# A planned attention and expert kernel: another model of transfers in its planner, and another order on each engine

## The chip, the cores and the metric

The kernel runs on one core of one Trainium2 chip. Time is device time in microseconds (us), from runs of the whole program on that core. Five engines work beside each other, each through its own list of instructions in order: TensorE (PE), VectorE (DVE), ScalarE (ACT), GpSimd (POOL) and SyncE (SP). SP computes nothing; it issues the loads from device memory. ACT issues the stores, between its own computations.

## The reference

The input `x` has 4 batches of 11456 tokens with 128 features; there are 32 inducing points and 8 experts. Cut to what matters:

```python
def mab(q, kv):                       # softmax attention
    s = scale * (q @ kv.T); a = softmax(s); return a @ kv
h   = mab(inducing, x)                # per batch: 32 points look at all tokens
out = mab(x, h)                       # per batch: all tokens look at the 32 points
# then a mixture of experts on every token of out
expert = argmax(normalised(out) @ normalised(expert_emb).T / tau)
y = gate_weight * (relu(out @ w1[expert]) @ w2[expert])
```

The second step of a batch needs all of that batch's `h`, and `h` needs every token of the batch. So each batch has a point at which everything waits for the last of its loads.

## The kernel before

A batch is cut into six pieces `k` of 2048 tokens (the last has 1280 here and overlaps). Each piece is loaded twice: `xT` (or `xL` for the last piece) holds features on the partitions, `x` holds tokens on the partitions, and a small `xR` holds the last rest of 192 tokens of a batch. Batch 0 makes three of its `x` pieces on PE instead of loading them.

Stage 1 of a batch (`stage1`) computes scores of the inducing points against the pieces (L495), their running maximum (L556, L563), exponentials on ACT (L571), transposes on PE (L594), and sums weighted rows of `x` (L617). `finish` joins the sums into `hT`, the transposed `h` of the batch, lets an expert be picked (`pick`) and has SP load that expert's two weight matrices (`get_w`, L753 and L754). Stage 2 (`stage2`) scores each piece against `hT` (L792), which is the last use of that piece's `xT` buffer, and makes the exponentials and two groups of sums (L363, with tiles `HB` and `gbd`). `gate` makes the gate weights. `fold` folds the expert's two matrices into one small matrix `L`. Stage 3 (`stage3`) multiplies by the gate weights on POOL (L1150), makes the output on PE (L1169), copies it out of PSUM on ACT (L1176) and stores it from ACT (L445).

The four batches overlap: stage 1 of batch b+1 is worked in between stages 2 and 3 of batch b. Buffers are rings: seven `xT` of 1024 KB, two `xL` of 640 KB, four `x` of 1024 KB, one `xR` of 96 KB. A load waits on SP until the oldest buffer of its ring is free, and everything behind it on SP waits as well. `ORDER` holds for each engine the order of the operations, by their numbers. At build time `Plan.run` walks through these lists with estimated durations and places each operation in time; from that it takes the PSUM banks and the number of zero products (`fill`, L1265, a product of the zero tile `wz`) that are put into PE's estimated idle times. The times themselves do not reach the chip: there an instruction starts when its semaphores allow it.

Lines of this program that the text below touches: L461 loads `xT` and `xL`, L474 loads `x`, L480 loads `xR`, L724 reads the picked expert into a register of SP, L1303 issues four zero products at the start. The ring sizes and the six kinds of loads:

```python
BUFS = dict(xT=7, xL=2, x=4, xR=1, s1=2, pt=1, e=10, hq=2, ...)
nc.sync.dma_start(new(b)[:, a:a + w], st.xT_src(o + a, w))              # L461
nc.sync.dma_start(new(b)[:, :n], xP[st.b, :, 16 * k:16 * k + n, :])     # L474
nc.sync.dma_start(new(st.xr), xR[st.b])                                 # L480
nc.tensor.matmul(ps_all[:, b], lhsT=wz[:, 0:P], rhs=wz, start=True, stop=True)   # L1265, a zero product
```

Of the kernel before, what the change touches and what calls it, by code (L numbers as in the profile page):

```python
# [18 lines left out]
PE = mybir.EngineType.PE  # L19
ACT = mybir.EngineType.Activation  # L20
DVE = mybir.EngineType.DVE
# [42 lines left out]
    PE=(15, 18, 16, 29, 24, 28, 52, 31, 26, 53, 38, 42, 66, 40, 76, 48, 55, 62, 50, 86, 3, 72, 64, 82, 89, 74, 93, 84, 96, 139, 101, 126,  # L64
# [8 lines left out]
    Activation=(22, 0, 30, 25, 19, 35, 36, 39, 23, 54, 45, 37, 59, 46, 60, 49, 69, 79, 63, 70, 80, 47, 61, 71, 73, 91, 81, 92, 83, 95,  # L73
# [10 lines left out]
    DVE=(20, 21, 17, 57, 33, 34, 2, 27, 32, 43, 44, 58, 67, 77, 41, 68, 78, 56, 87, 51, 88, 65, 90, 94, 4, 75, 85, 97, 98, 102, 127, 128,  # L84
# [12 lines left out]
    SP=(5, 6, 9, 7, 10, 14, 12, 8, 11, 13, 124, 137, 254, 256, 125, 241, 103, 138, 161, 216, 382, 369, 162, 217, 242, 255, 383, 370, 501,  # L97
        462, 486, 406, 348, 461, 487, 499, 407, 614, 627, 500, 615, 746, 706, 628, 593, 651, 731, 744, 652, 707, 732, 745, 838, 1018,
        1025,),
    Pool=(1, 133, 157, 170, 237, 176, 250, 178, 276, 180, 111, 114, 282, 184, 186, 116, 284, 190, 191, 286, 193, 290, 292, 296, 201, 209,  # L100
# [11 lines left out]
class Buf:  # L112


    def __init__(self, ring, n=1):
        self.ring = ring
        self.n = n
        self.left = 0
        self.free_at = 0.0
        self.at = None  # L120
        self.t = None
# [5 lines left out]

class Plan:
# [7 lines left out]


    RATE = 405e3
    LANES = 8
    LANDING = 1.5  # L140
    BEGIN = 1.7
# [7 lines left out]
    MOST = 16  # L149

# [57 lines left out]
    def ready_at(self, o, clock):  # L208
# [5 lines left out]
        if o.size and len(self.under_way) >= self.LANES:  # L214
            t = max(t, self.under_way[-self.LANES] + self.HOP)
# [26 lines left out]
    def run(self):  # L242
        clock = {e: 0.0 for e in ENGINES}
# [3 lines left out]
        rest = [0.0, 0.0]  # L247
        at = 0.0
        left = {e: [self.ops[i] for i in ORDER[e.name]] for e in ENGINES}
        order = []  # L250
        while any(left.values()):
# [15 lines left out]
            if o.size:  # L267

                go = max(0.0, o.end + self.BEGIN - at) * self.RATE
                at = max(at, o.end + self.BEGIN)  # L270
                low = min(go / 2, *rest)
                rest = [r - low for r in rest]
                rest = [max(0.0, r - (go - 2 * low)) for r in rest]
                q = 0 if o.eng == SP else 1
                rest[q] += o.size
                o.end = o.done = at + (rest[q] + min(rest)) / self.RATE + self.LANDING
                self.under_way += [o.done] * o.parts
# [11 lines left out]
            order.append(o)  # L289
        for o in order:  # L290
            if o.spare:
                bank, idle = o.spare
                self.fill(bank, min(self.MOST, int((idle - self.SPARE) / self.FILL)))
            o.fn()
# [41 lines left out]
def tile_attn_moe(ctx: ExitStack, tc: tile.TileContext, xT, xP, xR, indT, emb, tau, w1, w2, aux, outT):  # L336
# [296 lines left out]
    def finish(plan, st):  # L633
# [110 lines left out]
        st.do["vp"] = c(DVE, 0.25, vp, free=[b6])  # L744
# [240 lines left out]
    def fold(plan, st):  # L985
# [23 lines left out]
        def signs():  # L1009
            ss = small.tile([P, NCH], F32, name="ss")  # L1010
            nc.vector.tensor_reduce(ss, st.G, AX.X, ALU.add)
            t["pos"] = small.tile([P, NCH], F32, name="pos")
            nc.vector.tensor_scalar(t["pos"], ss, 0.0, None, ALU.is_ge)
            t["ss"] = ss
        o_s = c(DVE, 0.6, signs)

        def chosen():
            st.Gm = bat.tile([P, NCH, M], F32, name="Gm")
# [404 lines left out]
```

## Time and profile before

| | us |
|---|---|
| median of 3 runs | 204.05 (203.6 to 205.35) |
| the profiled execution | 203.44 |
| its span, first to last instruction | 201.5 |
| PE busy | 180.0 (89%) |
| VectorE busy | 156.6 (78%) |
| ScalarE busy | 128.0 (64%) |
| GpSimd busy | 104.5 (52%) |
| moved by DMA | 72.32 MB, 359 GB/s over the span |

The granted clock of PE is 0.988 over the span. The profile's time lies 1.94 us above its span, and 0.6 us below the median. Of the 72.32 MB, 48.13 MB are read and 23.72 MB written. A chain of waits is read from its end back; a window gives each engine's busy time and what the transfers moved.

### The profile page before, as it was taken

How to read it: one execution, taken by the hardware profiler on the slowest of the kernel's cores; microseconds unless marked ns; L12 is line 12 of the kernel's file. 1: busy time of each engine (PE TensorE's matmuls, PEld its weight loads, DVE VectorE, ACT ScalarE, POOL GpSimd, SP SyncE). 2: the span in 40 equal slices, each digit the busy share in tenths (PEclk: the TensorE clock that was granted, in tenths of full speed). 3: DMA queues.
4: the chain of work that ended last, by engine and by line, in shares of the span. 5: the costliest groups of instructions: out<-in, count | busy, mean ns of one | idle time of the engine just before them, and what ended most of it. 6: DMA issues, size and time to landing. Idle time of an engine off the chain costs nothing.

```text
span 201.5 us, 6512 instructions
## 1 busy us (share of the span) xinstructions
PE 180.0 (89%) x2568; PEld 90.3 (45%) x2568; DVE 156.6 (78%) x446; ACT 128.0 (64%) x305; POOL 104.5 (52%) x178
## 2 busy tenths in 40 slices
PE   7999999999996999995979998897899999999940
PEld 2466853653575453334634453354543333433310
DVE  6148627999977899787659999699489999878830
ACT  2066960756796647965665967688587799874400
POOL 3010000048874823686456177789665889987500
PEclk9999999999999999999999999999999999999995
DMA  6999999999999999999995999999767966688991
GB/s 198 424 420 379 415 410 361 347 419 421 413 415 423 321 352 394 434 412 426 417 419 185 425 371 365 422 428 425 304 246 300 378 259 264 259 332 333 390 415 39
DMA packets 12227, 72.32 MB, mean 359 GB/s; under 512 B 1624, under 2 KB 2144, under 8 KB 4896
## 3 DMA queue, kind: packets, MB, share of 16 engines
q1 hardware_dynamic: 7984, 48.12, 60.6%
q10 hardware_dynamic: 4208, 23.75, 28.7%
q8 instruction: 21, 0.34, 0.7%
q14 instruction: 14, 0.11, 0.2%
HBM read 48.13 MB, written 23.72 MB: 357 GB/s over the span
## 4 chain that ended last, share of the span: by engine, by line
PE 48%; DMA 34%; POOL 5%; DVE 3%; ACT 3%; issue 2%; ACTq 0%; POOLq 0%; DVEq 0%; SPq 0%
DMA x<-in_xP 19%; DMA xT<-in_xT 16%; PE ps L363 9%; PE ps L792 8%; PE ps L617 7%; PE ps L1169 6%; PE ps L495 5%; PE ps L1265 5%; PE ps L594 3%; PE ps L522 3%; POOL e L1150 2%; PE ps L1303 1%; ACT o L1176 1%; PE ps L1071 1%; DVE nn L834 1%
## 5 line engine op out<-in xcount | busy, mean ns | idle before, releaser
L830 POOL TENSOR_TENSOR hq<-hq,e 128x512 f32<-128x512 f32 (+1 forms) x24 | 29.1, 1216 | 42.7 <-ACT hq L826 42.7
L1176 ACT COPY o<-ps 128x512 f32<-128x512 f32 (+1 forms) x78 | 40.9, 567 | 10.0 <-PE ps L1169 9.0
L1150 POOL TENSOR_TENSOR e<-e,fb 128x512 f32<-128x512 f32 (+1 forms) x24 | 28.9, 1210 | 4.6 <-DVE fb L1146 2.4
L1169 PE MATMUL ps<-e,L 32*128 32x512 f32 (+1 forms) x192 | 26.0, 610 | 0.5 <-POOL e L1150 0.3
L617 PE MATMUL ps<-x,pt 128*32 128x128 f32 x608 | 20.8, 274 | 4.4 <-DMA x<-in_xP 4.1
L363 PE MATMUL ps<-e,gbd 128*32 128x256 f32 (+1 forms) x384 | 24.1, 367 | 0.1
L363 PE MATMUL ps<-e,HB 128*32 128x512 f32 (+1 forms) x192 | 24.0, 568 | 0.1
L571 ACT ACTIVATE s<-ps,nb 128x1024 f32<-128x1024 f32 (+3 forms) x15 | 13.4, 895 | 16.3 <-DVE nb L563 12.8
L495 PE MATMUL ps<-xT,indT_sb 128*32 128x512 f32 x160 | 20.8, 598 | 2.7 <-DMA xT<-in_xT 2.7
L556 DVE TENSOR_REDUCE mk<-ps 128x1 f32<-128x1024 f32 (+3 forms) x15 | 14.0, 939 | 11.7 <-PE ps L495 10.1
L792 PE MATMUL ps<-xT,hT 128*32 128x512 f32 x160 | 20.3, 596 | 0.1
L617 PEld LDWEIGHTS ps<-x,pt 128*32 128x32 f32 x608 | 16.4, 109 | 8.8 <-DMA x<-in_xP 3.0
L814 ACT ACTIVATE e<-e 128x512 f32<-128x512 f32 (+1 forms) x24 | 14.6, 608 | 8.0 <-DVE R L809 7.8
L1265 PE MATMUL ps<-wz 128*128 128x512 f16 x71 | 18.9, 401 | 0.1
L363 PEld LDWEIGHTS ps<-e,gbd 128*32 128x32 f32 x384 | 12.1, 110 | 13.4 <-issue 5.0
L826 ACT COPY hq<-ps 128x512 f32<-128x512 f32 (+1 forms) x24 | 13.3, 555 | 6.4 <-PE ps L363 5.8
L834 DVE TRANSPOSE_TENSOR_REDUCE nn<-hq 128x16 f32<-128x512 f32 (+1 forms) x24 | 15.8, 662 | 1.9 <-POOL hq L830 1.8
L798 DVE TRANSPOSE_TENSOR_REDUCE mx<-ps 128x16 f32<-128x512 f32 (+1 forms) x24 | 15.6, 662 | 1.5 <-PE ps L792 0.9
L1146 DVE STREAM_TRANSPOSE fb<-f 128x512 f32<-128x512 f32 (+1 forms) x24 | 15.6, 655 | 0.8 <-POOL f L975 0.6
L803 DVE STREAM_TRANSPOSE e<-mx 128x512 f32<-128x512 f32 (+1 forms) x24 | 15.3, 650 | 0.1
L809 DVE CUSTOM_DVE_ANT_0 e<-e,ps 128x512 f32<-128x512 f32 (+1 forms) x24 | 15.1, 631 | 0.2
L594 PE MATMUL ps<-ident,s 128*128 128x128 f32 (+1 forms) x92 | 13.2, 280 | 1.6 <-issue 1.6
(190 smaller groups left out, 307.2 us busy)
## 6 DMA issues: line engine op xcount, KB each, us to landing
xT<-in_xT SPq DMA_DIRECT2D x20, 1024.0 KB, 11.6
out<-o ACTq DMA_DIRECT2D x18, 1024.0 KB, 5.5
x<-in_xP SPq DMA_DIRECT2D x17, 1024.0 KB, 10.8
xL<-in_xT SPq DMA_DIRECT2D x4, 640.0 KB, 12.8
x<-in_xP SPq DMA_DIRECT2D x4, 512.0 KB, 17.3
w1t<-in_w SPq DMA_DIRECT2D x4, 512.0 KB, 6.1
w2t<-in_w SPq DMA_DIRECT2D x4, 512.0 KB, 6.8
out<-x ACTq DMA_DIRECT2D x2, 1024.0 KB, 6.2
```

The costliest lines, as they stand in the source:

```text
L363: nc.tensor.matmul(out[q:q + M], lhsT=lhsT[:, q:q + M], rhs=rhs, start=start, stop=stop)
L495: nc.tensor.matmul(ps[32 * j:32 * j + 32, :].rearrange("p (g i) -> p g i", i=128), lhsT=indT_sb, rhs=v[:, j], start=True, stop=True)
L594: nc.tensor.transpose(ps[:tw, q:q + 128], s1.t[:, at[k] + c0:at[k] + c0 + tw], ident)
L617: nc.tensor.matmul(ph.t[32 * j:32 * j + 32, 0:C], lhsT=pt.t[:tw, tat[k] + g, 32 * j:32 * j + 32], rhs=x, start=k == ks[0] and g == 0, stop ...
L792: nc.tensor.matmul(ps[32 * j:32 * j + 32, :W].rearrange("p (t i) -> p t i", i=32), lhsT=st.hT[:, 0:M], rhs=v[:, j], start=True, stop=True)
L798: nc.vector.tensor_reduce(new(mx)[:, :T], b1.t[:, :W].rearrange("p (t i) -> p t i", i=32), AX.X, ALU.max, apply_transpose=True)
L830: nc.gpsimd.tensor_tensor(paired(hq.t[:, :W]), paired(hq.t[:, :W]), halved(e.t[:, :W]), ALU.mult)
L834: nc.vector.tensor_reduce(new(nn)[:, t0:t0 + T], hq.t[:, :W].rearrange("p (t i) -> p t i", i=32), AX.X, ALU.add, apply_transpose=True)
L1150: nc.gpsimd.tensor_tensor(e.t[:, :W], e.t[:, :W], fb.t[:, :W], ALU.mult)
L1169: nc.tensor.matmul(new(pcs[j])[:, :W], lhsT=st.L[32 * j:32 * j + 32, :], rhs=pf.t[32 * j:32 * j + 32, :W], start=True, stop=True)
L1176: (nc.vector.tensor_copy if dve else nc.scalar.copy)(v[:, j], pcs[j].t[:, :W].rearrange("c (t i) -> c t i", i=32))
L1265: nc.tensor.matmul(ps_all[:, b], lhsT=wz[:, 0:P], rhs=wz, start=True, stop=True)
```

## The change

Three things change. First, the planner's model of transfers: a class `Transfers` keeps one queue for SP and one for ACT, gives each an equal share of a fixed rate, moves the estimated landing of all transfers under way whenever one is added, and adds a delay that grows with the time for which the transfers have been busy (at most 2.4 us), for sixteen transfer engines that drift apart. PE's planned time now starts at 3.1 us and SP's at 1.0. Second, the first place for zero products is divided by 0.4 us in place of 0.22, and PE's first idle time is shorter, so there are 7 products there in place of 16; with all later places the program has 63 zero products where it had 75. Two estimated durations on DVE change, and these two wait for POOL in the plan. Third, `ORDER` holds another order for every engine. No computation is added or taken away other than zero products, and no buffer or tile changes size. The numbers of `ORDER` tell a reader little; a line of SP's stands for the rest:

```diff
-    SP=(5, 6, 9, 7, 10, 14, 12, 8, 11, 13, 124, 137, 254, 256, 125, 241, 103, 138, ...
+    SP=(5, 6, 9, 7, 10, 12, 8, 11, 14, 13, 124, 137, 138, 125, 254, 216, 161, 103, ...
...
+class Transfers:
+    RATE = 424e3
+    BEGIN = (1.4, 0.6)
+    LANDING = 0.8
+    DRIFT = 0.1
+    APART = 2.4
+    def add(self, o, t):
+        self.run(t)
+        q = 0 if o.eng == SP else 1
+        self.queues[q].append([o, o.size, o.end + self.BEGIN[q]])
+        Transfers(self).run(1e6)
+    def run(self, to):
+        while self.now < to:
+            on = [q for q in self.queues if q and q[0][2] <= self.now + 1e-9]
...
+            rate = self.RATE / len(on)
+            step = min([to - self.now, begin - self.now] + [q[0][1] / rate for q in on])
+            self.now += step
+            for q in on:
+                q[0][1] -= rate * step
+                if q[0][1] < 1:
+                    o = q.pop(0)[0]
+                    o.end = o.done = self.now + self.LANDING + min(self.APART, self.DRIFT * (self.now - self.busy))
...
-    RATE = 405e3
     LANES = 8
-    LANDING = 1.5
-    BEGIN = 1.7
+    CLOCK = {PE: 3.1, ACT: 0.0, DVE: 0.0, SP: 1.0, POOL: 0.0}
...
+    FILL0 = 0.4
...
-                self.fill(bank, min(self.MOST, int((idle - self.SPARE) / self.FILL)))
+                self.fill(bank, min(self.MOST, int((idle - self.SPARE) / (self.FILL if filled else self.FILL0))))
+                filled = True
...
-        st.do["vp"] = c(DVE, 0.25, vp, free=[b6])
+        st.do["vp"] = c(DVE, 0.4, vp, free=[b6], port=True)
...
-        o_s = c(DVE, 0.6, signs)
+        o_s = c(DVE, 0.68, signs, port=True)
```

Three places show what moved. The first is SP, the loads of batch 1 behind the first two `xT` pieces of that batch, before:

```order
L461 DMA xT<-in_xT 128x2048 x2
L461 DMA xL<-in_xT 128x1280
L480 DMA xR<-in_xR 48x512
L474 DMA x<-in_xP 128x2048
L461 DMA xT<-in_xT 128x2048
L724 TENSOR_LOAD ei
```

and the same place now (`ei` is the picked expert; the lines are those of the changed file, 36 higher):

```order
L497 DMA xT<-in_xT 128x2048 x2
L510 DMA x<-in_xP 128x2048 x2
L497 DMA xL<-in_xT 128x1280
L497 DMA xT<-in_xT 128x2048 x2
L760 TENSOR_LOAD ei
```

The `xR` of batch 1 is gone from here: it now stands as the 25th of SP's operations where it was the 14th, just ahead of the last `x` piece of that batch. Two `x` pieces and two `xT` pieces stand ahead of the reading of the expert, where there were one of each. In batch 2 the `xR` moves the same way, from the 29th to the 39th place.

The second place is SP again, between the last `x` piece of batch 2 and the reading of batch 2's expert, before:

```order
L474 DMA x<-in_xP 128x1024
L474 DMA x<-in_xP 128x2048
L480 DMA xR<-in_xR 48x512
L461 DMA xT<-in_xT 128x2048
L474 DMA x<-in_xP 128x2048
L724 TENSOR_LOAD ei
```

and now:

```order
L510 DMA x<-in_xP 128x1024
L510 DMA x<-in_xP 128x2048
L497 DMA xL<-in_xT 128x1280
L510 DMA x<-in_xP 128x2048
L497 DMA xT<-in_xT 128x2048 x2
L516 DMA xR<-in_xR 48x512
L760 TENSOR_LOAD ei
```

The `xR` of batch 3 goes behind an `xL`, an `x` and two `xT` pieces; the `xL` and one `xT` stood behind the expert's weights before.

The third place is PE in the last batch, towards the end of its stage 2, before (`e` are exponentials, `HB` and `gbd` the tables of that batch, `L` the folded matrix of batch 2):

```order
L363 MATMUL ps<-pad_135,ones 32x1 x4
L363 MATMUL ps<-e,gbd_137 32x256 x8
L363 MATMUL ps<-pad_135,ones 32x1 x4
L363 MATMUL ps<-e,HB 32x320 x4
L1169 MATMUL ps<-e,L 128x512 x4
L363 MATMUL ps<-Lp,sel_124 32x128 x4
```

and now:

```order
L399 MATMUL ps<-e,HB 32x512 x4
L1205 MATMUL ps<-e,L 128x512 x4
L1301 LDWEIGHTS wz
L1301 MATMUL ps<-wz 128x512
L399 MATMUL ps<-pad_135,ones 32x1 x4
L399 MATMUL ps<-e,gbd_137 32x160 x8
L1091 MATMUL ps<-ident,wo 1x128
L399 MATMUL ps<-e,HB 32x320 x4
```

Zero products now stand between the stage 2 products of the last batch: four of them ahead of its last `HB` product, and eight more ahead of batch 2's last output product. Before, the first of them there came behind the last stage 2 product, 12 in one place.

More of the change, by code (lines that the diff above doesn't have):

```diff
@@ L63 @@
 ORDER = dict(
-    PE=(15, 18, 16, 29, 24, 28, 52, 31, 26, 53, 38, 42, 66, 40, 76, 48, 55, 62, 50, 86, 3, 72, 64, 82, 89, 74, 93, 84, 96, 139, 101, 126,
[8 rows of a table removed]
-    Activation=(22, 0, 30, 25, 19, 35, 36, 39, 23, 54, 45, 37, 59, 46, 60, 49, 69, 79, 63, 70, 80, 47, 61, 71, 73, 91, 81, 92, 83, 95,
[10 rows of a table removed]
-    DVE=(20, 21, 17, 57, 33, 34, 2, 27, 32, 43, 44, 58, 67, 77, 41, 68, 78, 56, 87, 51, 88, 65, 90, 94, 4, 75, 85, 97, 98, 102, 127, 128,
[12 rows of a table removed]
-    SP=(5, 6, 9, 7, 10, 14, 12, 8, 11, 13, 124, 137, 254, 256, 125, 241, 103, 138, 161, 216, 382, 369, 162, 217, 242, 255, 383, 370, 501,
-        462, 486, 406, 348, 461, 487, 499, 407, 614, 627, 500, 615, 746, 706, 628, 593, 651, 731, 744, 652, 707, 732, 745, 838, 1018,
-        1025,),
-    Pool=(1, 133, 157, 170, 237, 176, 250, 178, 276, 180, 111, 114, 282, 184, 186, 116, 284, 190, 191, 286, 193, 290, 292, 296, 201, 209,
[4 rows of a table removed]
+    PE=(15, 16, 18, 28, 29, 31, 53, 52, 24, 42, 26, 38, 55, 66, 40, 48, 76, 62, 50, 72, 86, 64, 82, 89, 74, 93, 84, 3, 96, 139, 126, 99,
[8 rows of a table added]
+    Activation=(19, 22, 35, 54, 25, 0, 30, 39, 36, 45, 23, 37, 59, 49, 46, 69, 60, 70, 47, 63, 61, 79, 80, 73, 71, 81, 91, 92, 83, 95,
[10 rows of a table added]
+    DVE=(20, 21, 17, 33, 34, 57, 43, 44, 58, 32, 2, 67, 68, 56, 27, 77, 41, 78, 87, 51, 88, 65, 90, 75, 94, 85, 4, 97, 127, 98, 128, 100,
[12 rows of a table added]
+    SP=(5, 6, 9, 7, 10, 12, 8, 11, 14, 13, 124, 137, 138, 125, 254, 216, 161, 103, 241, 369, 162, 382, 217, 242, 256, 255, 499, 370, 383,
+        407, 487, 461, 406, 486, 348, 614, 462, 627, 501, 500, 615, 744, 628, 706, 651, 746, 593, 731, 707, 652, 732, 745, 1018, 838,
+        1025,),
+    Pool=(1, 133, 170, 157, 237, 176, 250, 276, 178, 114, 111, 180, 282, 186, 184, 284, 116, 190, 191, 286, 193, 292, 296, 209, 290, 201,
[4 rows of a table added]
 )
@@ L125, with __init__ @@
     pass
+class Transfers:
[4 more added lines that the diff above has]
+    APART = 2.4
+    def __init__(self, other=None):
+        self.queues = [[list(x) for x in q] for q in other.queues] if other else [[], []]
+        self.now, self.busy = (other.now, other.busy) if other else (0.0, None)
+    def add(self, o, t):
[6 more added lines that the diff above has]
+            on = [q for q in self.queues if q and q[0][2] <= self.now + 1e-9]
+            begin = min([q[0][2] for q in self.queues if q and q not in on], default=1e9)
+            if not on:
+                self.busy = None
+                self.now = min(to, begin)
+                continue
+            if self.busy is None:
+                self.busy = self.now
+            rate = self.RATE / len(on)
[6 more added lines that the diff above has]
+                    o.end = o.done = self.now + self.LANDING + min(self.APART, self.DRIFT * (self.now - self.busy))
+                    for b in o.free:
+                        b.free_at = max(b.free_at, o.done)
 class Plan:
@@ L214, in ready_at @@
         if o.size and len(self.under_way) >= self.LANES:
-            t = max(t, self.under_way[-self.LANES] + self.HOP)
+            t = max(t, self.under_way[-self.LANES].done + self.HOP)
         o.room = 0.0
@@ L242, in run @@
     def run(self):
-        clock = {e: 0.0 for e in ENGINES}
+        clock = dict(self.CLOCK)
         self.pool_from = 0.0
@@ L246, in run @@
         self.under_way = []
-        rest = [0.0, 0.0]
-        at = 0.0
+        dma = Transfers()
         left = {e: [self.ops[i] for i in ORDER[e.name]] for e in ENGINES}
@@ L267, in run @@
             if o.size:
[L269 to L277, printed above, removed]
+                dma.add(o, t)
+                self.under_way += [o] * o.parts
             for b in o.take:
@@ L289, in run @@
             order.append(o)
+        filled = False
         for o in order:
```

68 rows, old and new, of tables (Activation, DVE, PE, Pool) are left out of this document.

## The prediction, made before the result

> **What bounds the kernel now.** I read the page's head first, then the chain of waits in order of time, the transfers by windows, and SP's waits.
>
> ```profile
> span 201.5 us, 6512 instructions
> ...
> DMA packets 12227, 72.32 MB, mean 359 GB/s; under 512 B 1624, under 2 KB 2144, under 8 KB 4896
> ```
>
> The chain (start, duration, what):
>
> ```profile
> 1.39 1.89 PE ps L1303 x4
> ...
> 35.53 13.24 DMA xT<-in_xT
> ...
> 76.63 8.91 DMA xT<-in_xT
> 85.56 19.05 DMA x<-in_xP
> ...
> 104.65 1.00 PE ps L617 x24
> ...
> 117.14 9.48 DMA xT<-in_xT
> 126.68 18.44 DMA x<-in_xP
> ...
> 145.17 1.00 PE ps L617 x24
> 146.17 1.06 PE ps L1169 x5
> ```
>
> From 35 us to 145 us the chain runs through loads three times, and each time it ends at the PE work that needs them: at 104.65 the last weighted rows of batch 2, at 145.17 those of batch 3. Behind 145.17 no load of `x` or `xT` is left, and 56.3 us of work for the last batch follow to the end of the span at 201.5. So the end moves with the landing of the last `x`, as far as the engines keep up.
>
> A transfer that takes 19 us isn't slow; it stands behind others. The windows (us from the span's start: length, busy us of PE, PEld, DVE, ACT, POOL with counts, granted clock, busy share of the transfer engines, GB/s) show whether the transfers were full:
>
> ```profile
> 2.00:28.00 26.00, 25.77 (x327) 15.89 (x324) 13.50 (x64) 14.84 (x37) 0.89 (x5) 1.00 1.01 400
> 28.00:38.00 10.00, 9.86 (x132) 4.29 (x132) 7.71 (x23) 2.42 (x5) 0.00 (x0) 1.00 0.96 354
> 38.00:66.00 28.00, 25.96 (x473) 16.04 (x477) 24.77 (x67) 19.97 (x50) 18.08 (x31) 1.00 1.01 416
> 66.00:68.00 2.00, 1.99 (x30) 0.68 (x26) 2.00 (x5) 2.00 (x4) 1.10 (x3) 1.00 0.86 229
> 68.00:106.00 38.00, 33.72 (x557) 17.24 (x549) 29.88 (x81) 24.97 (x59) 21.02 (x35) 1.00 1.01 407
> 106.00:112.00 6.00, 5.99 (x92) 2.31 (x84) 5.78 (x15) 3.60 (x10) 3.99 (x4) 1.00 0.64 220
> 112.00:142.00 30.00, 26.87 (x414) 13.99 (x410) 26.93 (x69) 22.25 (x52) 20.84 (x35) 1.00 1.01 404
> ```
>
> They were, at 400 to 416 GB/s, except in three places: 28 to 38, 66 to 68 and 106 to 112 us. SP's own waits and issues tell why (waits: us in total, times, longest):
>
> ```profile
> SPq L480 <- PE ps L617: 25.4, 3, 12.2
> ...
> SPq L474 <- DMA x<-in_xP: 15.8, 3, 9.7
> ```
>
> ```profile
> 16.50 0.33 SPq L461 DMA_DIRECT2D xL<-in_xT  x1
> 29.11 0.33 SPq L480 DMA_DIRECT2D xR<-in_xR  x1
> ...
> 65.62 0.33 SPq L480 DMA_DIRECT2D xR<-in_xR  x1
> ...
> 105.71 0.33 SPq L480 DMA_DIRECT2D xR<-in_xR  x1
> 108.59 0.34 SPq L461 DMA_DIRECT2D xT<-in_xT  x1
> ```
>
> The three waits of L480 are the `xR` loads of batches 1, 2 and 3. Their ring has one buffer, free only when the previous batch's last rows (L617) are through, and behind each the whole load queue stands still. The three thin places of the windows begin where these waits end or shortly before: the transfers in flight ran dry. That is the loss that this order can win back.
>
> **The change, part by part.** All sums are made against the profiled execution: 203.44 us, a span of 201.5 and 1.94 around it; the median of the three runs is 0.6 higher. I take 416 GB/s, the second window, as what full transfers move.
>
> *The `xR` of batch 1 moves from SP's 14th to its 25th place.* In the gap from 16.50 to 29.11 SP can now issue an `x` at once (batch 0 loads three `x` into a ring of four), the next `x` and the `xL` as buffers come free. The window 28 to 38 moved 354 where 416 go: 10 x (416 - 354) / 416 = 1.5 us.
>
> *The `xR` of batch 2 moves from the 29th to the 39th place.* Two further `x` pieces of batch 2 and then three `xT` stand in its stead; the `x` wait for batch 1's last rows, piece by piece, which end just ahead of 65.62. Window 66 to 68: 2 x (416 - 229) / 416 = 0.9 us.
>
> *The `xR` of batch 3 goes behind an `xL`, an `x` and two `xT`.* The `xL` needs a buffer that batch 1 left long before; 640 KB at 416 GB/s are 1.6 us of transfers. The `x` needs the rows that stand just ahead of the last ones of batch 2, the `xT` need its first scores (L792), which follow `hT`; so they fill the remainder, if not at once. Window 106 to 112: 6 x (416 - 220) / 416 = 2.8 us. The reading of the expert (L724) now stands behind these loads, and the weights land later; who waits is `fold` of batch 2, whose product `L` is wanted only by outputs in the last 56 us.
>
> Together 5.2 us by which the last `x` could land sooner. The same bytes stand ahead of the last load, and the stores are on the other queue. Can the engines follow? From 28 to 142 us the six windows from there hold 104.4 us of PE work and 97.1 of DVE in 114. Taking 5.2 us out leaves 108.8: PE 96% busy, DVE 89%. It fits, but nearly without slack, and every engine has a new order whose own waits no row of before shows. I bound what reaches the end by 0 (an engine takes the place of the transfers) and 5.2, and take 4.0, nearer the upper end, because PE waited on loads in this stretch and its idle 9.6 us are almost twice the gain.
>
> *Nine zero products fewer at the start.* The rows:
>
> ```profile
> 0.97 2.71 SPq L461 DMA_DIRECT2D xT<-in_xT  x5
> ...
> 5.21 0.15 PEld L1265 LDWEIGHTS <-wz 128*128 128x128 f16 x1 [0.28 <-issue]
> 5.58 1.83 PEld L1265 LDWEIGHTS <-wz 128*128 128x128 f16 x9 [0.21 <-issue]
> 7.83 1.06 PE L495 MATMUL ps<-xT,indT_sb 128*32 128x512 f32 x8
> ```
>
> ```profile
> DMA to landing us min/median/max: 5.1/5.1/5.1
> ```
>
> The last line is the first `xT` piece alone: issued at 0.97, landed at 6.1. PE was at its zero products until 7.83. The nine that go are those of the second row, begun at 5.58; so the seventh is the one begun at 5.21, and PE can score at 6.1, 1.7 us sooner. I cost this at nothing for the end: batch 0's further loads arrive in line, transfers were full from 2 to 28 us, and the loads that bound the chain later are not sooner for it. If that cover is gone (PE bound throughout), it is a gain of up to 1.7. What it might lose: the first ten products took from 1.39 to 5.21 to begin, 0.42 us each, and the nine 1.83 / 9 = 0.20 us each, so PE had gone to its fast pace at 5.58. That is before 6.1, so the first scores still find it fast. [...]
>
> *Zero products in the tail.* Four now stand between stage 2 products of the last batch, in a stretch in which PE was full:
>
> ```profile
> 160.00:170.00 10.00, 10.00 (x140) 3.67 (x140) 9.74 (x28) 9.33 (x23) 9.23 (x17) 1.00 0.64 263
> 172.15 2.76 PE L1265 MATMUL ps<-wz 128*128 128x512 f16 x12
> ```
>
> At 2.76 / 12 = 0.23 us they cost at most 0.9 us, nothing if PE waits there. I count nothing: DVE and ACT are as full in the window, and the first of them late makes PE wait.
>
> *All else.* The planner's new costs send no instruction to the chip. The moved worst-case check of batch 2, `put_h` stores of 64 KB and the order of POOL's gate steps have only the end of the kernel waiting for them; nothing, and up to 0.5 us either way.
>
> **The rivals.** *An engine takes the place of the transfers.* The loads land sooner, but the last 56 us grow by as much, because work that was done during the dry places is now still to do. For it: in the window 160 to 170 PE, DVE, ACT and POOL are all over 92%. Against it: PE's list of work behind the last rows of batch 3 is the same as before but for one group of output products (L1169, 1.06 us in the chain's last row). Only up to 1.5 us remain: 202.5 to 204.5, about 203.4.
>
> *Stores hold up ACT (slower).* A transfer may only be issued when the eighth before it has landed: this is what SP waits for in the row L474 <- DMA. Once SP no longer stands at `xR`, more transfers are in flight, and ACT, which issues the stores between its evictions, waits there too.
>
> ```profile
> out<-o ACTq DMA_DIRECT2D x7, 1024.0 KB, 9.9
> ...
> PEld ps L363 <- ACT o L1176: 6.4, 13, 1.1
> ```
>
> The first row is the stores from 28 to 142 us, and one of 608 KB goes with them; the second shows that PE does wait for ACT's evictions. 1024 KB at 416 GB/s are 2.5 us. If each of eight stores holds ACT for two such landings, that is 40 us; ACT is busy 75.2 of 114 us by the same windows, so 34% of it is hidden, and if PE sees a quarter of the rest, 6.6 us. Against the 4.0 gained: 203.44 + 2.6, or about 206.6 by the median. It decides from about 4 us that reach PE, half a microsecond per store. Against it: among ACT's waits of before none is for a transfer, though SP waited for a landing for up to 9.7 us.
>
> *It doesn't do what it says.* The transfers may be at their limit already: the page's head has a mean of 359 GB/s, and 72.32 MB at that rate fill the span. Then the dry places would fill and the rest thin out, and the time stays at 204.05. The 416 GB/s over 28 us speak against it. [...]
>
> **How the numbers follow.** Forecast: 203.44 - 4.0 = 199.4 for the profiled execution; the median stood 0.6 higher, so 200.0. Its own range is 197.1 (all of 5.2 and the 1.7 of the start) to 202.0.
>
> A change of over 1% is what a measurement of this kernel can tell from none, that is below 202.0 or above 206.1. The forecast has 0.58, all of it faster. An engine in the place of the transfers has 0.22, of it 0.03 faster. The stores have 0.14, slower, since the gain may be smaller too. The limit has 0.02, no change, and 0.04 are left for other mishaps of a new order: 0.01 no change, 0.03 slower. Faster 0.61, same 0.22, slower 0.17. The range for 8 in 10 takes in the forecast's lower end nearly whole and the first rival: 196.8 to 205.0; the stores and the tails stay outside.
>
> **What would show it.** Right: no wait of SP for `xR` above some 3 us; no window of 6 us before the last `x` lands under 350 GB/s; the last rows of batch 3 start at about 141 us where they started at 145.17, with about 56 us behind them. First score at 6.1 us. The first rival: the last rows at 141 but 59 us or more behind them. The stores: evictions (L1176) or PE waiting on ACT for over 10 us in sum. My forecast is wrong if the last `x` lands no sooner than 144, or if PE's waits from 28 to 142 us grow.

## The result, and the profile after

The changed kernel takes 198.15 us (median of 4 runs, 197.51 to 199.22), the kernel before 203.82 on the same chip (4 runs, 202.71 to 205.35). The ratio is 0.972, with a 95% interval of 0.965 to 0.980: 2.8% faster. (All ratios leave disturbed runs out, so a ratio can differ a little from that of the medians beside it.) The profiled execution took 197.51 us. The head of its page, and of its transfers:

```profile
span 195.7 us, 6482 instructions
...
DMA packets 12227, 72.32 MB, mean 369 GB/s; under 512 B 1624, under 2 KB 2144, under 8 KB 4896
```

The same 72.32 MB are moved at 369 GB/s over the span, where it was 359. The chain of waits of the changed kernel (start, duration, what; its lines are 36 higher, so L653 is the former L617):

```profile
0.97 5.44 DMA xT<-in_xT
...
57.66 8.74 DMA x<-in_xP
...
73.20 12.11 DMA kT<-hT
85.33 16.59 DMA x<-in_xP
101.97 1.00 PE ps L653 x24
...
120.88 18.13 DMA x<-in_xP
139.06 1.00 PE ps L653 x24
```

The chain still runs through loads to the last weighted rows of a batch. Those of batch 2 start at 101.97 (104.65 before), those of batch 3 at 139.06 (145.17 before), which is 6.1 us sooner. One link is new: the last `x` of batch 2 goes out at 85.33, on the landing of a 64 KB store of `h` that ACT issued at 73.20 (`kT<-hT`). The prediction took it that only the end of the kernel waits for these stores. No loss shows, since this `x` went out at 85.56 before. The span went from 201.5 to 195.7, 5.8 us shorter. Behind the last rows 195.7 - 139.06 = 56.6 us are left, where it was 56.3. So the whole gain is made ahead of 139 us, and the last batch's work took as long as before.

The windows (length, busy us of PE, PEld, DVE, ACT, POOL with counts, granted clock, busy share of the transfer engines, GB/s):

```profile
28.00:38.00 10.00, 9.62 (x124) 4.25 (x120) 7.39 (x20) 2.51 (x5) 0.00 (x0) 1.00 1.01 417
38.00:66.00 28.00, 26.54 (x501) 16.79 (x489) 26.27 (x72) 20.65 (x52) 19.43 (x32) 1.00 1.02 407
66.00:68.00 2.00, 1.17 (x32) 0.90 (x36) 1.02 (x2) 1.17 (x3) 1.11 (x3) 1.00 1.00 410
68.00:106.00 38.00, 36.06 (x571) 17.79 (x574) 33.31 (x87) 26.81 (x65) 21.32 (x37) 1.00 1.02 415
106.00:112.00 6.00, 6.00 (x102) 3.31 (x98) 5.93 (x15) 3.38 (x7) 2.24 (x2) 1.00 1.00 418
112.00:142.00 30.00, 28.09 (x474) 14.46 (x463) 27.30 (x74) 24.01 (x60) 24.22 (x41) 1.00 0.97 389
```

The three dry places are gone: 354 became 417, 229 became 410, 220 became 418 GB/s. In these 114 us PE is now busy for 107.5 (104.4 before), so its idle time there fell from 9.6 to 6.5 us. What SP waits for (us in total, times, longest):

```profile
SPq L510 <- DMA xT<-in_xT: 13.5, 7, 4.5
SPq L497 <- PE ps L828: 12.9, 5, 5.3
SPq L510 <- DMA x<-in_xP: 10.4, 3, 4.6
```

The row for `xR` waiting on the last rows, 25.4 us in three waits before, is no longer there; the one wait left at an `xR` (L516) is 0.9 us. The `xT` loads (L497) now wait for the products that free their buffers, and the `x` loads (L510) for an earlier transfer to land, which the prediction names as the eighth before. At two places it was: the `x` of 85.33 went out on the landing of the store issued at 73.20, with seven loads issued between them, and in the kernel before the `x` of 85.56 on that of the `xT` issued at 76.63, with five loads and two stores between.

### The profile page after: what moved, and what is told of

Read it like the earlier page. It is cut to its first block, busy times and chain, and to the rows that moved or that the text cites. A ratio compares the mean times of both kernels' runs of the same rounds, so it can differ in the third digit from the quotient of the medians.

```text
span 195.7 us, 6482 instructions
## 1 busy us (share of the span) xinstructions
PE 178.0 (91%) x2556; PEld 89.9 (46%) x2556; DVE 157.0 (80%) x446; ACT 127.9 (65%) x305; POOL 104.2 (53%) x178
## 2 busy tenths in 40 slices
DMA packets 12227, 72.32 MB, mean 369 GB/s; under 512 B 1624, under 2 KB 2144, under 8 KB 4896
## 4 chain that ended last, share of the span: by engine, by line
DMA 40%; PE 31%; POOL 12%; DVE 8%; issue 3%; ACT 3%; ACTq 0%; DVEq 0%; POOLq 0%; SPq 0%
DMA x<-in_xP 22%; DMA xT<-in_xT 11%; DMA kT<-hT 6%; PE ps L399 6%; PE ps L653 5%; PE ps L828 4%; PE ps L531 4%; POOL e L1186 4%; PE ps L1205 4%; POOL hq L866 3%; PE ps L558 3%; PE ps L630 3%; DVE mx L834 2%; PE ps L1301 1%; DVE e L839 1%
## 5 line engine op out<-in xcount | busy, mean ns | idle before, releaser
L1212 ACT COPY o<-ps 128x512 f32<-128x512 f32 (+1 forms) x78 | 40.0, 567 | 11.8 <-PE ps L1205 11.2
L653 PE MATMUL ps<-x,pt 128*32 128x128 f32 x608 | 21.6, 275 | 3.7 <-ACT zs L618 1.6
L399 PE MATMUL ps<-e,gbd 128*32 128x256 f32 (+1 forms) x384 | 23.3, 367 | 0.0
L531 PE MATMUL ps<-xT,indT_sb 128*32 128x512 f32 x160 | 21.2, 598 | 2.2 <-DMA xT<-in_xT 2.2
L653 PEld LDWEIGHTS ps<-x,pt 128*32 128x32 f32 x608 | 16.7, 109 | 8.0 <-issue 2.6
L1301 PE MATMUL ps<-wz 128*128 128x512 f16 x59 | 15.9, 397 | 0.0
```

The source lines that it names most:

```text
L399: nc.tensor.matmul(out[q:q + M], lhsT=lhsT[:, q:q + M], rhs=rhs, start=start, stop=stop)
L531: nc.tensor.matmul(ps[32 * j:32 * j + 32, :].rearrange("p (g i) -> p g i", i=128), lhsT=indT_sb, rhs=v[:, j], start=True, stop=True)
L653: nc.tensor.matmul(ph.t[32 * j:32 * j + 32, 0:C], lhsT=pt.t[:tw, tat[k] + g, 32 * j:32 * j + 32], rhs=x, start=k == ks[0] and g == 0, stop ...
L1212: (nc.vector.tensor_copy if dve else nc.scalar.copy)(v[:, j], pcs[j].t[:, :W].rearrange("c (t i) -> c t i", i=32))
```

## The experiments

In each, except where the edit is to the zero products themselves, their number at every place is held at that of the kernel it starts from, so that only the edit differs. The numbers in the edits are SP's operations: 256 and 501 are the `xR` of batches 1 and 2, 255 and 500 the last `x` piece of each, 746 the `xR` of batch 3.

**The third place alone (e2_third).** The kernel before, with the changed order between batch 2's last `x` and batch 3:

```diff
-    SP=(... 500, 615, 746, 706, 628, 593, 651, 731, 744, 652, ...
+    SP=(... 500, 615, 744, 628, 706, 651, 746, 593, 731, 652, ...
```

> The kernel before, with SP's order changed only between the last x of batch 2 and the third last x of batch 3, where it takes the order of the changed kernel (xL, x, two xT, xR, expert weights, xT). Theory: the dry place at 106 to 112 us fills, worth 2.8 us; 1.5 to 3.5 us faster than before, about 201. Rival (the orders of the computing engines bring the gain): within 1 us of before, the dry place filled or moved but the end unmoved.

It took 200.62 us (199.83 to 201.56) beside 203.63, ratio 0.986 (0.978 to 0.994), 2.9 us faster. Its window, and its last rows of batch 3 from the chain:

```profile
106.00:112.00 6.00, 5.99 (x74) 2.61 (x74) 5.82 (x15) 3.76 (x10) 3.98 (x4) 1.00 1.02 420
```

```profile
141.58 1.00 PE ps L617 x24
```

The place went from 220 to 420 GB/s, and the last rows came 3.6 us sooner in this execution. The term of 2.8 us is about right: 3.6 by this landing, 2.9 by the times.

**The `xR` of batches 1 and 2 alone (e1_two_xr).** They move to just ahead of the last `x` piece, and nothing else does:

```diff
-    SP=(... 124, 137, 254, 256, 125, ... 242, 255, ... 370, 501, 462, ... 627, 500, ...
+    SP=(... 124, 137, 254, 125, ... 242, 256, 255, ... 370, 462, ... 627, 501, 500, ...
```

> The kernel before, with SP's order changed in two loads alone: the xR of batch 1 and the xR of batch 2 stand just ahead of the last x piece of their batch, as in the changed kernel. All other orders, the planner and the zero products are those of before. Theory (dry transfers behind a waiting xR): the dry places at 28 to 38 and 66 to 68 us fill, worth 1.5 and 0.9 us; so 1 to 3 us faster than before, about 201.4, and the last x lands as much sooner. Rival (the new orders of the computing engines bring the gain): within 1 us of before.

It was slower: 206.03 us (205.91 to 208.65), ratio 1.015 (1.005 to 1.025). Neither side of the expectation held, and the trace shows two things that went wrong. First its chain and SP's issues:

```profile
76.39 11.64 DMA x<-in_xP
88.05 17.42 DMA x<-in_xP
...
147.61 1.00 PE ps L617 x24
```

```profile
85.43 0.33 SPq L480 DMA_DIRECT2D xR<-in_xR  x1
```

Before, an `xT` issued at 76.63 landed 8.91 later, at 85.54, and batch 2's last `x` went out at 85.56, on that landing. Here the small `xR` goes out at 85.43 in its stead, and the last `x` has to wait for the next landing, 76.39 + 11.64 = 88.03: it goes out at 88.05, 2.5 us later. It lands 0.9 us later (105.47 for 104.61). Now PE (first row, with the pause ahead of it in brackets) and the windows behind it, the clock being the number third from the end:

```profile
105.51 0.65 PE L617 MATMUL ps<-x,pt 128*32 128x128 f32 x16 [2.58 <-DMA x<-in_xP]
```

```profile
28.00:38.00 10.00, 9.87 (x136) 4.19 (x128) 7.74 (x21) 2.72 (x6) 0.00 (x0) 1.00 0.98 382
...
106.00:112.00 6.00, 6.00 (x87) 2.50 (x83) 3.88 (x12) 1.47 (x3) 3.59 (x4) 0.72 0.34 119
```

```profile
107.00:108.00 1.00, 1.00 (x23) 0.59 (x19) 0.86 (x4) 0.66 (x2) 0.00 (x0) 0.62 0.57 188
108.00:110.00 2.00, 2.00 (x26) 0.88 (x29) 1.55 (x7) 0.81 (x2) 1.59 (x2) 0.50 0.12 41
```

PE paused for 2.58 us where it was 1.10, and 1.7 us after it began again its granted clock fell to half (0.62 over the first microsecond is half clock from about 107.24 on). That is where PE makes `hT` and the first products against it, which free the buffer that the next `xT` waits for. The first place has 382 GB/s for 354 (but 372 in e2_third, which leaves this place as it was, so that this window by itself shows little), while the third became worse than before, 119 for 220, and the last rows came at 147.61, 2.4 us late. The length of the pause does not explain this alone: the last section has one of 2.74 us that left the clock at 1.00.

**Both together (e9_all_xr).** The two edits above in one kernel. If the late third place ate the gain, filling it should bring it back:

> The kernel before with the two moves of the xR loads of e1_two_xr and the third place of e2_third together; all else as before. e1_two_xr was 2.4 us slower, and the question is why. Theory: the transfers won at the first two places were given back in the third, where the queue stood still longer (119 GB/s from 106 to 112 us, 220 before) and PE's granted clock fell to 0.72 there; with the third place filled nothing is left to give back, so at least as good as e2_third: 200.6 or below, down to 198.5, with 106 to 112 us above 350 GB/s and the last x of batch 3 landing by 141. Rival: the small load directly ahead of the last x piece takes one of the eight places in line, makes that x later and costs its 2.4 us wherever the third place stands: about 203.0, with last rows of batch 2 at 105.5 or later.

It took 201.80 us (201.22 to 202.50), ratio 0.988 (0.982 to 0.995). Windows, two successive issues of SP, and the last rows of batches 2 and 3:

```profile
28.00:38.00 10.00, 9.77 (x143) 4.07 (x137) 7.01 (x20) 3.03 (x8) 0.00 (x0) 1.00 0.89 337
...
106.00:112.00 6.00, 5.99 (x95) 2.34 (x88) 5.78 (x15) 3.31 (x10) 3.98 (x4) 1.00 1.02 422
```

```profile
16.88 0.43 SPq L474 DMA_DIRECT2D x<-in_xP  x1
32.69 0.33 SPq L461 DMA_DIRECT2D xT<-in_xT  x1
```

```profile
104.73 0.64 PE L617 MATMUL ps<-x,pt 128*32 128x128 f32 x16 [1.50 <-DMA x<-in_xP]
```

```profile
143.10 1.00 PE ps L617 x24
```

The loss is gone, but so is any gain: 2.4 us faster than before is no more than the 2.9 that the third place alone brings. The first place is not filled (337 GB/s here, 382 with the same loads above, 354 before): SP goes past the place of `xR`, issues one `x` at 16.88 and then stands at the next `xT` until 32.69, whose buffer a product has to free. Neither side of the expectation holds whole. Filling the third place takes the loss away, as the theory said, but not down to its 200.6; the rival's loss of 2.4 us did not come, nor its late rows of batch 2. Here too the small `xR` put off that batch's last `x` (it went out at 89.01), yet the last rows began at 104.73, PE paused for 1.50 us and the clock stayed at 1.00. With the third place alone they began at 103.79, so the put-off costs at most about 1 us; the rest of e1_two_xr's loss goes with the longer pause and the half clock behind it, as far as these single traces show.

**The first place, whole (f1_first, f2_first_third).** So it should be the `x` pieces ahead of the waiting `xT` that fill it. SP's 16 operations from batch 1's first `xT` to its last `x` piece in the changed order, on the kernel before:

```diff
-    SP=(... 124, 137, 254, 256, 125, 241, 103, 138, 161, 216, 382, 369, 162, 217, 242, 255, ...
+    SP=(... 124, 137, 138, 125, 254, 216, 161, 103, 241, 369, 162, 382, 217, 242, 256, 255, ...
```

> The kernel before with SP's order of after at the first place alone: the 16 loads from batch 1's first xT to its last x piece, so that two x pieces, an xL and an xT stand where the xR stood, and the xR just ahead of the last x. (Moving the xR alone left SP standing at the next xT until 32.7 us and the window from 28 to 38 at 337 GB/s in e9_all_xr.) Theory: what fills this place is not the xR's absence but x pieces whose buffers are free; 28 to 38 us above 400 GB/s, worth the 1.5 us of the sum: 202.2, between 201.5 and 203. Rival: a stall filled early is given back at the third place, which keeps its xR wait: 203.6 or more, as e1_two_xr at 206, with 106 to 112 us under 220 GB/s.

It took 201.49 us (200.81 to 202.47) beside 204.22, ratio 0.991 (0.987 to 0.995), 1.9 us faster:

```profile
28.00:38.00 10.00, 9.86 (x132) 4.29 (x132) 7.70 (x23) 2.42 (x5) 0.00 (x0) 1.00 1.01 418
...
106.00:112.00 6.00, 5.93 (x74) 2.69 (x70) 5.75 (x17) 3.46 (x9) 3.19 (x3) 1.00 0.80 293
```

```profile
16.51 7.47 SPq L474 DMA_DIRECT2D x<-in_xP  x2
```

```profile
142.61 1.00 PE ps L617 x24
```

Two `x` pieces (the row of SP's issues) and then the `xL` now go out ahead of the waiting `xT`; in e9_all_xr it was the `xL` and one `x`. The place is full at 418 GB/s, and nothing was given back at the third, which still waits for its `xR` (293 GB/s, 220 before). With the edit of the third place added:

> f1_first and the third place of e2_third together; the second place (batch 2's xR and its neighbours) as before. Theory: the places add up as in the sum: 200.6 less 1.5 is 199.1, and the second place is the rest to the 198.0 of e3_sp_order, with 66 to 68 us still under 300 GB/s. Rival: the first place is worth nothing without the second: 200.6 or more.

198.72 us (198.38 to 200.35), ratio 0.981 (0.972 to 0.989), 4.0 us faster, with the second place and the last rows at:

```profile
66.00:68.00 2.00, 2.00 (x36) 1.03 (x32) 1.48 (x5) 0.91 (x2) 2.00 (x2) 1.00 1.02 338
```

```profile
140.07 1.00 PE ps L617 x24
```

The time is near the theory's 199.1, but the second place is not as thin as it said (under 300 GB/s): it has 338 without its own edit, 229 before.

**All of SP's order, and nothing else (e3_sp_order).** The kernel before with SP's changed list; PE, VectorE, ScalarE and GpSimd keep their old orders, the zero products and the planner too.

```diff
-    SP=(5, 6, 9, 7, 10, 14, 12, 8, 11, 13, 124, 137, 254, 256, ...
+    SP=(5, 6, 9, 7, 10, 12, 8, 11, 14, 13, 124, 137, 138, 125, ...
```

> The kernel before with the whole order of SP from the changed kernel; PE, ACT, DVE and POOL keep their orders, zero products as before. Theory: all three dry places fill, about 5 us faster than before (3 to 6), 198 to 200.5. Rival: the other engines' old orders need loads in the old sequence, so PE stands waiting for loads that are now later: no gain, or slower by up to 5 us.

198.04 us (197.92 to 198.12), ratio 0.972 (0.965 to 0.978): the whole gain of the change. Its last rows, and the longest pause of PE in that stretch:

```profile
139.55 1.00 PE ps L617 x24
```

```profile
95.39 1.08 PE L617 MATMUL ps<-x,pt 128*32 128x128 f32 x32 [2.23 <-DMA x<-in_xP]
```

**The waits taken away, the order kept (e10_ring2).** The kernel before with two `xR` buffers; `Lp`, `G` and `Gm` of `fold` have one buffer in place of two, to make room:

```diff
-BUFS = dict(xT=7, xL=2, x=4, xR=1, ...
+BUFS = dict(xT=7, xL=2, x=4, xR=2, ...
```

> The kernel before with two xR buffers in place of one (and one buffer in place of two for Lp, G and Gm of fold, to make room); the order of every engine as before. This takes away what xR waits for, not its place. Theory: the waits for xR are the loss in the first two places, so they fill (over 395 GB/s from 28 to 38 and over 350 from 66 to 68 us), worth 1.5 + 0.9 us; in the third the next load, an xT, still waits for the first scores against hT until about 108, so that stays under 330 GB/s: 201.2, between 200 and 202.5. Rival, by the slower e1_two_xr: filling the first two places alone only shifts the stall to the third, and the time is 203 to 206, with the last rows of batch 2 no sooner than 104.6.

202.36 us (200.49 to 204.35), ratio 0.988 (0.976 to 0.999), 2.5 us faster, though its interval only just leaves out 1, with:

```profile
28.00:38.00 10.00, 9.87 (x136) 4.32 (x137) 7.70 (x23) 2.47 (x6) 0.00 (x0) 1.00 0.99 377
...
66.00:68.00 2.00, 1.96 (x30) 0.83 (x30) 2.00 (x6) 2.00 (x5) 1.08 (x3) 1.00 1.06 341
...
106.00:112.00 6.00, 5.99 (x74) 2.61 (x74) 5.82 (x15) 3.77 (x10) 3.98 (x4) 1.00 0.73 256
```

```profile
143.78 0.99 PE ps L617 x24
```

The time lies within the theory's 200 to 202.5 and below the rival's 203 to 206, but the windows are not what the theory asked. The first place, at 377, hardly differs from the 354 of before and the 372 of e2_third, the second has 341 for 229, and in the third the next load, an `xT`, waits as foreseen. SP issues the `xR` at 16.75 and an `x` at 18.17 and then stands at the next `xT` until 31.89, as in e9_all_xr: the wait for `xR` was only the first of several in line. Which place the 2.5 us come from is not shown.

**The other engines' orders with the old loads (e4_old_sp, e11_old_sp_ring2).** The changed kernel with SP's order of before, and then the same with two `xR` buffers:

```diff
-    SP=(5, 6, 9, 7, 10, 12, 8, 11, 14, 13, 124, 137, 138, 125, ...
+    SP=(5, 6, 9, 7, 10, 14, 12, 8, 11, 13, 124, 137, 254, 256, ...
```

> The changed kernel with the order of SP from before; the other four engines keep the new orders, zero products as in the changed kernel. Theory: the dry places come back, 4 to 7 us slower than the changed kernel, 202 to 205, that is about the time before. Rival: the new orders of the computing engines hold the gain: 198 to 200.

> e4_old_sp (the changed kernel with SP's order of before) with two xR buffers in place of one (and one buffer for Lp, G and Gm). Theory: what e4_old_sp lost (212.0) is that the other engines' new orders expect loads that stand behind a waiting xR; without that wait most of the loss goes: 203 to 206. Rival: the engines' orders wait for the xT and x loads in another order than SP issues them, whatever xR does: 209 or more, with PE still waiting for xT (L531) for over 6 us.

The first took 212.01 us (209.57 to 214.06), ratio 1.036 (1.026 to 1.046), far slower than the kernel before, which was not expected. The second took 211.07 (209.20 to 214.36), ratio 1.033 (1.022 to 1.045). So it isn't the wait for `xR`: the rival's 209 or more came, though hardly its sign: PE's waits for `xT` at L531 are 3.4 us in sum, not over 6. The second one's windows, and its last rows of batch 3 in the timeline:

```profile
68.00:106.00 38.00, 31.23 (x454) 15.12 (x453) 29.28 (x75) 23.48 (x56) 19.30 (x30) 0.96 0.93 364
...
112.00:142.00 30.00, 27.02 (x378) 12.21 (x370) 24.64 (x66) 19.07 (x42) 17.27 (x25) 0.94 0.90 340
```

```profile
149.91 0.62 PE L653 MATMUL ps<-x,pt 128*32 128x128 f32 x16
```

The transfers run dry over long stretches (364 and 340 GB/s, 407 and 404 before), not in three spots, and the last rows come 4.7 us later than in the kernel before. That fits engines which take the pieces in the order of the new load list: with the old one they come to a piece late and free its buffer late, and the loads wait for it. The granted clock, 0.96 and 0.94 in these windows where it was 1.00, may have a part in it. This cause is argued from the traces; which engine's order does most of it was not tried.

**The planner alone (e5_planner).** The changed planner, with the durations and the PSUM banks that come out of it, and the orders and zero products of before:

```diff
 ORDER = dict(
-    PE=(15, 16, 18, 28, 29, 31, 53, ...
+    PE=(15, 18, 16, 29, 24, 28, 52, ...
```

> The changed planner (new model of transfers, new durations, and the PSUM banks that come out of it) with the orders and the zero products of before. The prediction counted this at nothing: 203.6 within 1 us. Rival: other banks let PE start sooner or later where it waits for a bank to be copied out: 2 us or more either way.

It took 205.37 us (202.06 to 208.55, ten runs) beside 204.23. The ratio is 0.998 (0.992 to 1.003): nothing that can be told from noise, as the prediction had it, though these runs spread wider than those of before (202.88 to 206.99). Whether the transfer engines drift apart, as the planner's model takes it, these times do not show.

**The zero products (e7_16_zero, f4_tail_zero).** The changed kernel with 16 in the first place instead of 7, and the changed kernel without the 12 in the last batch (`ZEROS` holds the counts by the operation that follows):

```diff
-    ZEROS = {15: 7, ...}
+    ZEROS = {15: 16, ...}
```

> The changed kernel with 16 zero products in PE's first idle time, as before, in place of 7. Theory: first score at about 7.8 us in place of 6.5, and nothing at the end: 198.1 within 0.6. Rival: PE bounds from the start: up to 1.7 us more, 199.9.

```diff
-    ZEROS = {..., 950: 3, 840: 1, 798: 3, 806: 5, ...}
+    ZEROS = {..., 950: 0, 840: 0, 798: 0, 806: 0, ...}
```

> The changed kernel without the 12 zero products between the last batch's stage 2 products and ahead of batch 2's last outputs (the prediction spoke of the first four). Theory: PE waits there for the other engines, so they cost nothing: 198.1 within 0.6. Rival 1: PE is full there, and 12 x 0.23 = 2.8 us go: 195.4, or 0.9 for the first four. Rival 2: without them PE's granted clock falls below 0.97 in the last 54 us, and it is slower by 1 us or more.

They took 197.23 us (196.39 to 198.61), ratio to before 0.971 (0.964 to 0.978), and 197.18 us (196.92 to 198.46), ratio 0.971 (0.965 to 0.977). The changed kernel has 0.972: neither edit can be told from it. With 16, the first score began at 7.20 us, and with the 7 of the changed kernel at 6.54:

```profile
7.20 1.07 PE L532 MATMUL ps<-xT,indT_sb 128*32 128x512 f32 x8
```

```profile
6.54 1.06 PE L531 MATMUL ps<-xT,indT_sb 128*32 128x512 f32 x8 [1.03 <-DMA xT<-in_xT]
```

In the last batch the changed kernel (first row) and the one without the 12 (second) differ in how busy PE is, 13.90 and 12.42 us of 14, and pauses stand where the products stood; the granted clock is 1.00 in both, so the second rival's slower clock did not come there:

```profile
156.00:170.00 14.00, 13.90 (x165) 5.64 (x158) 12.92 (x38) 12.44 (x31) 13.07 (x25) 1.00 0.74 303
```

```profile
156.00:170.00 14.00, 12.42 (x153) 5.56 (x146) 12.90 (x39) 12.38 (x31) 13.08 (x25) 1.00 0.74 304
```

No edit gave a version that is measurably faster than the changed kernel.

## Why the prediction was right

**What bounds it: right, and more exactly than claimed.** The prediction said that the end moves with the landing of the last `x`. The profiled execution's time less the start of batch 3's last rows is:

| kernel | profiled us | last rows | left |
|---|---|---|---|
| before | 203.44 | 145.17 | 58.3 |
| third place | 199.83 | 141.58 | 58.3 |
| two `xR` moved | 205.91 | 147.61 | 58.3 |
| two `xR` moved, and third | 201.53 | 143.10 | 58.4 |
| first place | 201.12 | 142.61 | 58.5 |
| first and third | 198.38 | 140.07 | 58.3 |
| SP's order | 197.92 | 139.55 | 58.4 |
| changed kernel | 197.51 | 139.06 | 58.5 |

Faster or slower, each kernel that keeps one set of orders on the computing engines ends 58.3 to 58.5 us behind that one point, and so does the other set in the changed kernel. (With two `xR` buffers it is 201.69 - 143.78 = 57.9, with the orders that don't match the loads 209.20 - 149.91 = 59.3, and in the changed kernel with 16 zero products first 198.39 - 139.75 = 58.6, without the 12 in the last batch 197.76 - 138.75 = 59.0.)

**The three dry places: the sum right, its parts roughly.** 1.5 + 0.9 + 2.8 = 5.2 us was forecast for the last rows. With SP's order alone they came 145.17 - 139.55 = 5.6 sooner, in the changed kernel 6.1. By place: the third alone 3.6 (forecast 2.8), the first alone 2.6 (1.5), both together 5.1 (4.3), and the second place takes it from 140.07 to 139.55, 0.5 (0.9). The places are not independent: 3.6 and 2.6 make 6.2, not 5.1, since the first place's edit alone lifts the third from 220 to 293 GB/s and the second from 229 to 327. In whole times, by the ratios, it is 2.9, 1.9, 4.0 and 5.8 in the same order; the intervals of the last two overlap, so the second place's own share isn't settled.

**The step that was off: taking 4.0 out of 5.2.** The discount was for engines whose new orders might not follow. They lost nothing: the tail is 56.6 us against 56.3, and with the old orders the time is the same (198.04 and 198.15). The forecast of 200.0 is 1.85 us above the 198.15 measured; 1.2 of it is this discount, and 0.9 that the last rows came 6.1 instead of 5.2 us sooner, less 0.2 of a longer stretch behind them (58.5 for 58.3). Where the 0.9 beyond the three windows comes from was not traced. The other signs held: no wait for `xR` over 0.9 us, and no 6 us before the last `x` lands under 359 GB/s (114.5 to 120.5 us).

**The cause: half right.** The prediction put the loss on the waiting `xR` and listed the loads that take its place. Moving the two `xR` of batches 1 and 2 without those loads brought 2.4 us of loss by itself and nothing on top of the third place. A load list in order has the next load behind the waiting one, and that one, an `xT`, waited until 32.69 as well. The prediction did name the `x` pieces with free buffers for the first place, and f1_first shows that these, with the `xL`, ahead of the waiting `xT` fill it.

**"All else" at nothing: right together with the new loads, wrong as a rule.** The planner (0.998) and the new orders of the other engines on top of the new loads bring nothing. But these orders with the old loads cost 7.3 us by the ratio (0.036 x 203.6). They belong to the load list, and the prediction, which weighed them only as a risk to the gain, did not say so.

**The zero products: right.** The first score came at 6.54 us rather than 6.1, since the first `xT` took 5.44 us to land rather than 5.1. The first eight scores took 1.06 us, as they did behind nine products more. The 0.66 us that the two counts put between the first scores moved the end by nothing measurable. The 12 in the last batch cost nothing either: PE waits there without them.

**The rivals.** Engines in the place of the transfers would have shown 59 us or more of tail; there are 56.6. Stores holding up ACT would have shown PE waiting for evictions. The waits of the changed kernel:

```profile
ACT o L1212 <- PE ps L1205: 11.2, 10, 5.3
...
PEld ps L399 <- ACT o L1212: 3.4, 8, 0.8
```

In the stage 2 products PE's weight loads wait for ACT's evictions for 3.4 us in sum where it was 6.4; over all of PE's rows it is 8.5 where it was 10.8. The evictions wait for PE (11.2 us, 9.0 before), not for a transfer. The transfers' limit, a mean of 359 GB/s, is refuted by 417 GB/s in the first place and 418 in the third. Of the steps that the prediction costed at nothing, the later reading of batch 2's expert was not tried by itself.

## What to carry to other kernels

In a queue that issues in order, moving one waiting load helps only if the next one can go: the `xR` moved alone left the first place at 382 and 337 GB/s, and two `x` pieces and the `xL` ahead of the waiting `xT` brought it to 418. So put ahead of the waiting load those whose buffers are already free, and look in the windows whether the place has filled. Find the point from which the rest of the kernel is a fixed stretch (58.3 us here), and judge each edit at that point. Orders of the computing engines belong to the order of the loads: exchange them together, and don't read the worth of one from a kernel that has the other's partner.

## What the runs showed of the hardware

In e1_two_xr a pause of PE of 2.58 us was followed by a granted clock of 0.62 and then 0.50 from 107 to 110 us. The work at half clock came on top of the pause: the rows behind the pause began 0.86 us later than in the kernel before (105.51 for 104.65), and the next `xT`, which waited for that work, went out 2.36 us later (110.95 for 108.59). The length of a pause did not decide this alone. In e11_old_sp_ring2 pauses of 2.26 and 2.31 us were followed by a clock of 0.57 (71 to 75 us) and 0.58 (133 to 137 us), while a pause of 2.23 us with SP's order alone, and one of 2.74 us with the first and third places, left it at 1.00. The last of these, and the window behind it:

```profile
91.38 0.64 PE L501 MATMUL ps<-xL,indT_sb 128*32 128x256 f32 x8 [2.74 <-DMA xL<-in_xT]
```

```profile
91.00:98.00 7.00, 6.45 (x136) 4.83 (x137) 4.78 (x14) 4.33 (x12) 4.74 (x6) 1.00 1.02 422
```

What decides besides the length is not shown.

A transfer's size did not matter for its turn in e1_two_xr: the `xR` of 96 KB that went out on a landing at 85.43 put off the 512 KB behind it by 2.6 us, to the next landing at 88.03.
